# Attention scores as tiles of 128 queries of one head, two heads on TensorE's row halves

## The chip, the cores and the metric

One core of a Trainium2 chip runs the whole program. The metric is the device time of one execution in microseconds, the median of three runs. A change of 0.2% is about what such a measurement can tell from no change.

## The reference

Three layers follow each other, all in float32:

```python
# attention: q, k, v of (batch 4, heads 8, sequence 576, width 64)
scores = (1/8) * q @ k.T
mask = block_i >= block_j            # blocks of 64: a query sees its own block and those before
attn = softmax(where(mask, scores, -1e9))
x = (attn @ v), heads side by side   # 2304 tokens x 512
# squared-ReLU layer, 512 -> 2048 -> 512
r = max(x @ w_in, 0);  x2 = (s * r * r + b) @ w_out
# top-1 mixture of 8 experts, 512 -> 1024 -> 512, chosen by modality-biased logits
out = gate * (max(x2 @ w1[e], 0) @ w2[e])
```

Products with full float32 accuracy are made of three passes: either operand is split into a high and a low part of the reduced type fp32r (names ending in h and l), and high by high, high by low and low by high are summed in PSUM (`PASSES`).

## The kernel before, in words

`attention` (line 21) works through 16 units; one unit is a batch's pair of heads. For each unit q and k come in as rows, are transposed on TensorE (`transpose4`, line 82; the last 64 rows in `tails`, line 113), copied out by ScalarE as the high part and subtracted by VectorE to the low part (`q_high`, `k_transpose`, `flush`).

The 576 queries of a unit are nine blocks of 64. `scores(u, i)` (line 123) makes one tile for block i: its 128 rows are 64 queries of the first head and the same 64 of the second. The stationary operand is block-diagonal (head 0's queries on rows 0 to 63, head 1's on rows 64 to 127, zeros elsewhere), so one full-array product gives both heads. The tile ends at the block's own edge, n = 64 (i + 1) keys, and needs no mask. The first two blocks are float32 products (line 137), the others three passes of fp32r of at least 256 columns (line 140), the ninth in two parts of 288. VectorE takes the row maximum (line 142), ScalarE the exponential with its sum (line 147).

```python
LAGS = (1, 5, 7)        # steps to normalise, p_transpose, pv
NPBUF = 6
BANKS_0 = (4, 3, 1)     # PSUM banks: scores, transposes, outputs
```

A step is one block. In step t `normalise` (line 151) for the block before takes the reciprocals on VectorE and multiplies on GpSimd (line 160); `p_transpose` (line 162) for the block five steps back turns the probabilities on TensorE (line 179) and ScalarE copies them out (line 185); `pv` (line 189) for a group of blocks makes the output, either head on one half of TensorE's columns (line 202), and ScalarE copies it out (line 204). A program-wide scheduler puts the instructions of all of this in an order for each engine.

`SquaredRelu` fills the rest. In the first stage its weights are converted, a chunk every few steps (`CONV`; VectorE lines 329 to 331, ScalarE 363, GpSimd 335). From step `PIECE_0` on, pieces of its first layers (`hidden`, line 376; `project`, line 391, sums in `pxa`) go between the attention's steps, one each `PIECE_D` steps, for tokens whose attention is done. What is left of the layer, the routing and the experts follow after the attention.

Of the kernel before, what the change touches and what calls it, by code (L numbers as in the profile page):

```python
# [20 lines left out]
def attention(nc, tc, ctx, ps, ident, q, k, v, xT_d):  # L21
    """x^T = softmax(mask(q k^T / 8)) v, written to xT_d[(head d), (batch s)]; a
    generator that yields (units finished) after each block of queries it emits.

    One unit is a batch's pair of heads.  Rows of the score tiles are a block of
    64 queries of either head (block-diagonal stationary), so a tile ends at its
    block's edge and needs no mask.
    """
    B, H, S, D = q.shape
    NB = S // D  # L30
# [14 lines left out]
    qb, qf = [], []  # L45
    for par in range(2):
        qq = []
        for nm in ("qh", "ql"):
# [3 lines left out]
        qb.append(qq)  # L52
        t = fix.tile([P, 2, 2, D], F32, name=f"qf{par}")
        nc.gpsimd.memset(t, 0.0)
        qf.append(t)
    st = {}
    todo = []

    def load(u, which):
# [4 lines left out]
        for nm, src in which:  # L64
            t = (vp if nm == "v" else raw).tile([P, 5, 2, D], F32, name=f"raw_{nm}", tag=nm)
            for hh in range(2):
                nc.sync.dma_start(t[:, 0:4, hh], src[b, h0 + hh, 0:512].rearrange("(c p) d -> p c d", p=P))
            ps.last["load"] = nc.sync.dma_start(t[0:D, 4], src[b, h0:h0 + 2, 512:].rearrange("h p d -> p h d"))
            ts.append(t)
# [18 lines left out]
    def q_high(u, src, blocks):  # L88
        skip = max(2 - blocks.start, 0)
        for hh in range(2):  # L90
            r = slice(hh * D, hh * D + D)
            a = src[r].rearrange("p (i d) -> p i d", d=D)
            if skip:
                nc.scalar.activation(qf[u % 2][r, :, hh], a[:, 0:skip], AF.Copy, scale=0.125)
                a = a[:, skip:]
            oh, ol = (t[r, blocks.start + skip - 2:blocks.stop - 2, hh] for t in qb[u % 2])
            nc.scalar.activation(oh, a, AF.Copy, scale=0.125)
            low(True, ol, a, oh)

    def q_transpose(u):  # L100
        q_high(u, transpose4(st[u]["raw"][0]), slice(0, 8))

    def k_transpose(u):
        kh = kt.tile([P, S], F32R, name="kh", tag="kh")
        kl = kt.tile([P, S], F32R, name="kl", tag="kl")
        kf = kt.tile([P, P], F32, name="kf", tag="kf")
        st[u]["k"] = (kh, kl, kf)
        t = transpose4(st[u]["raw"][1])
        nc.scalar.copy(kf, t[:, 0:P])
        nc.scalar.copy(kh[:, 0:512], t)  # L110
        low(False, kl[:, 0:512], t, kh[:, 0:512])

    def tails(u):
# [4 lines left out]
        q_high(u, t[:, 0:D], slice(8, 9))  # L118
        kh, kl, _ = st[u]["k"]
        nc.scalar.copy(kh[:, 512:], t[:, D:2 * D])  # L120
        low(False, kl[:, 512:], t[:, D:2 * D], kh[:, 512:])

    def scores(u, i):
        kh, kl, kf = st[u]["k"]
        qh, ql = qb[u % 2]
        n = (i + 1) * D
        pr = pp.tile([P, 640], F32, name="p", tag="p")
        if i % 2 == 0:
            nc.gpsimd.memset(pr[:, n:n + D], 0.0)
        parts = [(0, n)] if i < 8 else [(0, 288), (288, 288)]  # L130
        nm = small.tile([P, 2], F32, name="nm", tag="nm")
        sm = small.tile([P, 2], F32, name="sm", tag="sm")
        scs = []
        for e, (k0, w) in enumerate(parts):
            sc = ps.s.tile([P, 512], F32, name="sc", tag="s")
            if i < 2:
                nc.tensor.matmul(sc[:, 0:w], qf[u % 2][:, i].rearrange("p h d -> p (h d)"), kf[:, 0:w],
                                 start=True, stop=True)
            for j, (a, kk) in enumerate(((qh, kh), (qh, kl), (ql, kh)) if i >= 2 else ()):
                nc.tensor.matmul(sc[:, 0:max(w, 256)], a[:, i - 2].rearrange("p h d -> p (h d)"),  # L140
                                 kk[:, k0:k0 + max(w, 256)], start=(j == 0), stop=(j == 2))
            ps.last["max"] = nc.vector.tensor_reduce(nm[:, e:e + 1], sc[:, 0:w], AX.X, ALU.max, negate=True)  # L142
            scs.append(sc)
        if len(parts) == 2:
            nc.vector.tensor_tensor(nm[:, 0:1], nm[:, 0:1], nm[:, 1:2], ALU.min)
        for e, (k0, w) in enumerate(parts):
            ps.last["exp"] = nc.scalar.activation(pr[:, k0:k0 + w], scs[e][:, 0:w], AF.Exp, bias=nm[:, 0:1],  # L147
                                                  accum_out=sm[:, e:e + 1])
        st[u][i] = (pr, sm, len(parts))

    def normalise(u, i):
        n = (i + 1) * D
        pr, sm, k_ = st[u][i]
        rc = small.tile([P, 1], F32, name="rc", tag="rc")
        if k_ == 2:
            nc.vector.tensor_scalar(rc, sm[:, 0:1], sm[:, 1:2], 1e-9, ALU.add, ALU.add)
        else:
            nc.vector.tensor_scalar_add(rc, sm[:, 0:1], 1e-9)
# [3 lines left out]
    def p_transpose(u, blocks):  # L162
# [23 lines left out]
        for i in blocks:  # L186
            st[u].pop(i)
# [36 lines left out]
    for t in range(len(seq) + LP + 1):  # L224
# [26 lines left out]
        if i == 3:  # L251
            pv(u, 0)
# [956 lines left out]
```

## Time and profile before

| what | value |
|---|---|
| time, median of 3 runs | 957.22 us (956.84 to 957.99) |
| span of the profiled execution | 951.0 us |
| TensorE (PE) busy | 902.0 us, 95% |
| VectorE (DVE) busy | 593.8 us, 62% |
| ScalarE (ACT) busy | 521.1 us, 55% |
| GpSimd (POOL) busy | 252.3 us, 27% |
| last x^T of the attention sent off | 336.1 us |

The profile has no time of its own for this execution beside the span; the rest of the run's time lies before the first and behind the last instruction. Times are from the span's start. PE is TensorE's products, PEld its weight loads. An instruction's duration holds the time in which it drains, so two that follow each other overlap in the profile, and the step from one start to the next tells what it costs in a dense stream.

### The profile page before, as it was taken

To read this page: it belongs to the slowest core of one execution; us is meant where nothing else is said; L and a number is where in the kernel's file an instruction comes from. 1 tells how busy PE (TensorE), PEld (TensorE's weight loads), DVE (VectorE), ACT (ScalarE), POOL (GpSimd) and SP (SyncE) were. 2 spreads that over 40 slices of the span, in tenths; PEclk is the share of its full clock that TensorE was granted. 3 is DMA by queue.
4 is the path that set the end of the run, shared out by engine and by line. 5 is a ranking of instruction groups with operands and counts; after the bars stand their busy time and mean duration, and the time that the engine had idled before them with its cause. 6 is when DMAs were issued, how large, how long until landed. Compare 5 with 4: busy or idle time off the path is not lost. (4 is left out here: it accounts for less than half of the span.)

```text
span 951.0 us, 16300 instructions
## 1 busy us (share of the span) xinstructions
PE 902.0 (95%) x5553; PEld 728.7 (77%) x5553; DVE 593.8 (62%) x1340; ACT 521.1 (55%) x1105; POOL 252.3 (27%) x343
## 2 busy tenths in 40 slices
PE   7979999999999998999999999999779999999995
PEld 5666777888888887789898988887557776776774
DVE  5898886464546278743434444445877887676762
ACT  6878785566766443322222222224267877776763
POOL 4566674232323224200000000005251222222110
PEclk9999999999999999999999999999889999999998
DMA  6565643322220255200011222115162696637400
GB/s 146 153 155 138 177 131 80 89 57 67 73 70 27 79 180 163 71 21 26 20 32 40 64 67 67 45 46 202 42 246 84 238 372 234 225 121 255 170 24 25
DMA packets 105061, 107.50 MB, mean 113 GB/s; under 512 B 62359, under 2 KB 78249, under 8 KB 104971
## 3 DMA queue, kind: packets, MB, share of 16 engines
q1 hardware_dynamic: 101163, 94.45, 31.7%
q0 software_dynamic: 3808, 11.94, 3.5%
q8 instruction: 46, 0.75, 0.3%
q14 instruction: 44, 0.36, 0.1%
HBM read 139.38 MB, written 17.70 MB: 165 GB/s over the span
## 5 line engine op out<-in xcount | busy, mean ns | idle before, releaser
L376 PE MATMUL ph<-xh,wih 128*128 128x256 f32 x576 | 163.1, 283 | 0.0
L376 PE MATMUL ph<-xh,wil 128*128 128x256 f32 x576 | 162.5, 282 | 0.0
L376 PE MATMUL ph<-xl,wih 128*128 128x256 f32 x576 | 162.3, 282 | 0.0
L160 POOL TENSOR_TENSOR p<-p,rc 128x64 f32<-128x64 f32 (+2 forms) x144 | 111.8, 783 | 135.8 <-DVE rc L159 68.7
L380 ACT ACTIVATE r<-ph 128x512 f32<-128x512 f32 x72 | 43.0, 598 | 184.1 <-PE ph L376 158.0
L381 DVE SCALAR_TENSOR_TENSOR r<-r,sc 128x512 f32<-128x512 f32 x72 | 56.9, 792 | 112.8 <-ACT r L380 108.9
L376 PEld LDWEIGHTS ph<-xh,wih 128*128 128x128 f32 x576 | 109.1, 189 | 3.6 <-ACT r L380 0.9
L376 PEld LDWEIGHTS ph<-xl,wih 128*128 128x128 f32 x576 | 109.2, 190 | 2.2
L376 PEld LDWEIGHTS ph<-xh,wil 128*128 128x128 f32 x576 | 109.3, 190 | 0.2
L142 DVE TENSOR_REDUCE nm<-sc 128x1 f32<-128x288 f32 (+8 forms) x160 | 70.7, 450 | 53.7 <-PE sc L140 43.3
L147 ACT ACTIVATE p<-sc,nm 128x288 f32<-128x288 f32 (+8 forms) x160 | 80.6, 507 | 23.2 <-DVE nm L142 9.3
L885 DVE TENSOR_TENSOR w2l<-raw,w2h 128x1024 fp32r<-128x1024 f32 x62 | 79.9, 1303 | 14.6 <-ACT w2h L883 13.2
L391 PE MATMUL px<-woh,gh 128*128 128x512 f32 x200 | 82.6, 413 | 3.3 <-ACT gh L384 3.3
L391 PE MATMUL px<-woh,gl 128*128 128x512 f32 x200 | 79.3, 397 | 0.8 <-DVE gl L385 0.8
L885 DVE TENSOR_TENSOR w1l<-raw,w1h 128x1024 fp32r<-128x1024 f32 x58 | 70.0, 1226 | 15.7 <-ACT w1h L883 14.3
L391 PE MATMUL px<-wol,gh 128*128 128x512 f32 x200 | 79.3, 396 | 0.0
L883 ACT CAST w1h<-raw 128x1024 fp32r<-128x1024 f32 x64 | 65.7, 1050 | 22.1 <-PE ph L924 20.8
L883 ACT CAST w2h<-raw 128x1024 fp32r<-128x1024 f32 x64 | 66.6, 1051 | 12.4 <-PE py L940 11.7
L384 ACT ACTIVATE gh<-r,sc 128x512 fp32r<-128x512 f32 x72 | 52.1, 724 | 35.9 <-DVE r L381 35.7
L179 PE MATMUL tp<-ident,p 128*128 128x128 f32 x400 | 66.3, 281 | 5.3 <-POOL p L160 3.7
L894 POOL DMA_INDIRECT xr<-x_d,gidx_e x2 | 2.3, 1132 | 254.1 <-DMA raw<-in_moe_w_dram 253.8
L385 DVE SCALAR_TENSOR_TENSOR gl<-r,sc,gh 128x512 fp32r<-128x512 f32 x72 | 56.0, 778 | 20.8 <-ACT gh L384 20.4
(269 smaller groups left out, 2018.9 us busy)
## 6 DMA issues: line engine op xcount, KB each, us to landing
raw<-in_moe_w_dram SPq DMA_DIRECT2D x172, 512.0 KB
wr<-in_moe_w_in_dram SPq DMA_DIRECT2D x16, 512.0 KB
wr<-in_moe_w_out_dram SPq DMA_DIRECT2D x16, 512.0 KB
xr<-xT_d SPq DMA_DIRECT2D x15, 512.0 KB
x_d<-row SPq DMA_DIRECT2D x18, 256.5 KB
xT_d<-x SPq DMA_DIRECT2D x16, 288.0 KB
raw_q<-in_q_dram SPq DMA_DIRECT2D x32, 128.0 KB
raw_k<-in_k_dram SPq DMA_DIRECT2D x32, 128.0 KB
```

The lines of the kernel that those rows point to most:

```text
L142: ps.last["max"] = nc.vector.tensor_reduce(nm[:, e:e + 1], sc[:, 0:w], AX.X, ALU.max, negate=True)
L147: ps.last["exp"] = nc.scalar.activation(pr[:, k0:k0 + w], scs[e][:, 0:w], AF.Exp, bias=nm[:, 0:1], accum_out=sm[:, e:e + 1])
L160: ps.last["scale"] = nc.gpsimd.tensor_mul(pr[:, 0:n], pr[:, 0:n], rc.to_broadcast([P, n]))
L179: nc.tensor.transpose(t[:, e * P:(e + 1) * P], st[u][i][0][:, c * P:(c + 1) * P], ident)
L376: nc.tensor.matmul(ph[:, e], self.wi[p][w][:, c, e * P:(e + 1) * P], x[a][:, c], start=(n == 0), stop=(n == 3 * KC - 1))
L380: nc.scalar.activation(r, ph, AF.Relu)
L381: nc.vector.scalar_tensor_tensor(r, r, self.sc[:, 0:1], r, ALU.mult, ALU.mult)
L384: nc.scalar.activation(gh, r, AF.Identity, bias=self.sc[:, 1:2])
L385: nc.vector.scalar_tensor_tensor(gl, r, self.sc[:, 1:2], gh.bitcast(F32), ALU.add, ALU.subtract)
L391: self.nc.tensor.matmul(px, g[a][:, e, t * P:(t + 1) * P], self.wo[p][w][:, e], start=(first and e == 0 and n == 0), stop=(last and e == 1 ...
L883: self.nc.scalar.copy(ws[0][c], r)
L885: eng.tensor_sub(ws[1][c], r, ws[0][c].bitcast(F32))
```

## The change

The 576 queries become four tiles of 128 queries and one of 64. A tile of 128 (j = 0 to 3) is of one head: head 0 uses rows 0 to 63 of the array, head 1 rows 64 to 127, each with its own PSUM bank, and both are handled by one maximum and two exponentials. Keys run to n = 128 (j + 1); the later 64 queries of a tile see them all, the earlier 64 must not see the last 64, so a product of two small bf16 constants adds -1e30 there. The last 64 queries stay as before, one block-diagonal tile, now with one maximum and one exponential over both parts. A unit is 5 steps instead of 9. The float32 blocks, the copies for them, and the zeros behind odd tiles are gone; fp32r products of 128 columns are new. Output products and transposes have the same columns in another layout. Some copies of transposed probabilities go to VectorE from unit 4 on. A score tile takes two banks, so the FFN's `pxa` shares the bank of the outputs, and its sum is made in two pieces.

```diff
-            t = fix.tile([P, NB - 2, 2, D], F32R, name=f"{nm}{par}")
+            t = fix.tile([P, 2, D], F32R, name=f"{nm}{par}")
+    mq = fix.tile([P, P], BF16, name="mq")
+    mk = fix.tile([P, D], BF16, name="mk")
+    for hh in range(2):
+        nc.gpsimd.memset(mq[hh * D:hh * D + 1, 0:D], -1e30)
+        nc.gpsimd.memset(mk[hh * D:hh * D + 1], 1.0)
...
     def q_transpose(u):
-        q_high(u, transpose4(st[u]["raw"][0]), slice(0, 8))
+        qh = kt.tile([P, SF], F32R, name="qh", tag="qh")
+        ql = kt.tile([P, SF], F32R, name="ql", tag="ql")
+        st[u]["q"] = (qh, ql)
+        t = transpose4(st[u]["raw"][0])
+        nc.scalar.activation(qh, t, AF.Copy, scale=0.125)
+        low(True, ql, t, qh)
...
+    def scores(u, j):
+        kk, qq = st[u]["k"], st[u]["q"]
+        n = (j + 1) * P
+        pr = pp.tile([P, 2, 512], F32, name="p", tag="p")
...
+        sc = ps.s.tile([P, 2, 512], F32, name="sc", tag="s")
+        if j < NT:
+            for e, (a, w) in enumerate(PASSES):
+                for hh, r in enumerate(half):
+                    nc.tensor.matmul(sc[:, hh, 0:n], qq[a][r, j * P:(j + 1) * P], kk[w][r, 0:n],
+                                     start=(e == 0), stop=False)
+            for hh, r in enumerate(half):
+                nc.tensor.matmul(sc[:, hh, n - D:n], mq[r], mk[r], start=False, stop=True)
+            ps.last["max"] = nc.vector.tensor_reduce(nm, sc[:, :, 0:n], AX.X, ALU.max, negate=True)
+            for hh in range(2):
+                ps.last["exp"] = nc.scalar.activation(pr[:, hh, 0:n], sc[:, hh, 0:n], AF.Exp, bias=nm[:, hh:hh + 1],
+                                                      accum_out=sm[:, hh:hh + 1])
+            st[u][j] = (pr[:, :, 0:n], pr, sm)
         else:
...
+            ps.last["max"] = nc.vector.tensor_reduce(nm[:, 0:1], sc[:, :, 0:w_], AX.XY, ALU.max, negate=True)
...
-        ps.last["scale"] = nc.gpsimd.tensor_mul(pr[:, 0:n], pr[:, 0:n], rc.to_broadcast([P, n]))
+        ps.last["scale"] = nc.gpsimd.tensor_mul(pr, pr, rc.rearrange("p (g o) -> p g o", o=1).to_broadcast([P, g, n]))
...
-LAGS = (1, 5, 7)
-NPBUF = 6
+LAGS = (1, 3, 4)
+NPBUF = 4
 PTBUF = 1
-BANKS_0 = (4, 3, 1)
-P_COPY = lambda nc, i: nc.scalar.copy
+BANKS_0 = (2, 3, 1)
+P_COPY = lambda nc, u, j, e: nc.vector.tensor_copy if u >= 4 and j in (2, 4) and e else nc.scalar.copy
...
-                px = self.ps_x.tile([P, D], F32, name="pxa", tag="x")
+                px = self.ps_x.tile([P, D], F32, name="pxa", tag="o")
                 for p in range(n):
+                    if p == 2:
+                        yield blk
...
-BANKS_A = (3, 2, 1)
+BANKS_A = (2, 2, 1)
-CONV = [8 + 4 * n for n in range(19)]
-PIECE_0 = 50
-PIECE_D = 2.8
+CONV = [4 + 2 * n for n in range(19)]
+PIECE_0 = 26
+PIECE_D = 1.2
```

How it moves instructions: first TensorE in the first stage, transposes of probabilities (tp) and score products (sc), before:

```order
L179 MATMUL tp<-ident,p 128x128 x4
L140 MATMUL sc<-kh,qh_136 128x320
L140 MATMUL sc<-kl,qh_136 128x320
L179 MATMUL tp<-ident,p 128x128
L140 MATMUL sc<-kh,ql_138 128x320
L140 MATMUL sc<-kh,qh_136 128x384
```

The same place of the program after the change (mq and mk are the mask's constants):

```order
L188 MATMUL tp<-ident,p 128x128 x8
L134 MATMUL sc<-kh,qh 128x256 x2
L134 MATMUL sc<-kl,qh 128x256 x2
L134 MATMUL sc<-kh,ql 128x256 x2
L137 LDWEIGHTS mq
L137 MATMUL sc<-mk,mq 128x64
L137 LDWEIGHTS mq
L137 MATMUL sc<-mk,mq 128x64
L188 MATMUL tp<-ident,p 128x128 x4
L188 MATMUL tp<-ident,p 64x128
L134 MATMUL sc<-kh,qh 128x384 x2
```

Before, transposes and scores are all products on the full array; now the pairs (x2, one a head) and the mask stand on halves of its rows, between transposes on all rows and, for the tile's last 64 keys, one on half of the columns.

Second, ScalarE at the program's start (qf, qh, kf, kh: copies of q and k; p: exponentials), before:

```order
L97 ACTIVATE qh_136<-te 64x64 x2
L120 CAST kh<-te 128x64
L94 ACTIVATE qf_146<-tw 64x2x64
L97 ACTIVATE qh_142<-tw 64x6x64
L94 ACTIVATE qf_146<-tw 64x2x64
L97 ACTIVATE qh_142<-tw 64x6x64
L147 ACTIVATE p,sm<-sc,nm 128x64
```

And after:

```order
L118 ACTIVATE qdh_144<-te 64x64 x2
L121 CAST kh<-te 128x64
L140 ACTIVATE p,sm<-sc,nm 128x128 x2
L100 ACTIVATE qh<-tw 128x512
L140 ACTIVATE p,sm<-sc,nm 128x256 x2
```

The second unit's q copies stood ahead of the first exponential; now they stand behind it.

## Rows read from the trace of the kernel before

**Rows 1.** The page's head.

```profile
span 951.0 us, 16300 instructions
```

**Rows 2.** Busy time by stretch: us of the stretch, each engine, clock, DMA share, GB/s.

```profile
0.00:30.00 30.00, 23.56 (x135) 17.70 (x136) 18.83 (x71) 21.93 (x74) 15.20 (x37) 1.00 0.52 119
30.00:95.00 65.00, 56.86 (x391) 42.86 (x390) 57.41 (x173) 53.76 (x170) 41.53 (x68) 0.97 0.61 161
95.00:158.00 63.00, 59.19 (x421) 47.13 (x420) 50.84 (x153) 47.41 (x146) 41.98 (x66) 1.00 0.53 145
158.00:345.00 187.00, 186.77 (x1274) 153.96 (x1273) 94.42 (x279) 113.92 (x316) 53.80 (x96) 1.00 0.24 70
```

**Rows 3.** TensorE in order of time, saturated stage: start, us, instruction, count.

```profile
204.62 0.39 PE L140 MATMUL sc<-kl,qh 128*128 128x512 f32 x1
204.85 0.39 PE L140 MATMUL sc<-kh,ql 128*128 128x512 f32 x1
205.08 0.60 PE L179 MATMUL tp<-ident,p 128*128 128x128 f32 x4
...
205.65 0.29 PE L140 MATMUL sc<-kl,qh 128*128 128x288 f32 x1
205.78 0.29 PE L140 MATMUL sc<-kh,ql 128*128 128x288 f32 x1
...
212.22 0.33 PE L137 MATMUL sc<-kf,qf 128*128 128x64 f32 x2
212.39 0.50 PE L179 MATMUL tp<-ident,p 128*128 128x128 f32 x3
...
213.04 0.87 PE L202 MATMUL o<-pt,raw_v 128*64 128x256 f32 x8
213.85 0.66 PE L179 MATMUL tp<-ident,p 128*128 128x128 f32 x4
...
214.46 0.28 PE L140 MATMUL sc<-kl,qh 128*128 128x256 f32 x1
214.58 0.28 PE L140 MATMUL sc<-kh,ql 128*128 128x256 f32 x1
```

**Rows 4.** TensorE in order of time where two 64-row transposes interrupt FFN products.

```profile
180.36 0.38 PE L376 MATMUL ph<-xh,wih 128*128 128x256 f32 x1
180.67 0.27 PE L116 MATMUL te<-ident,raw_q 64*128 64x64 f32 x1
180.78 0.22 PE L116 MATMUL te<-ident,raw_k 64*128 64x64 f32 x1
180.94 0.38 PE L376 MATMUL ph<-xl,wih 128*128 128x256 f32 x1
181.16 0.28 PE L376 MATMUL ph<-xh,wil 128*128 128x256 f32 x1
```

**Rows 5.** TensorE's weight loads in order of time.

```profile
65.47 0.47 PEld L179 LDWEIGHTS tp<-ident,p 128*128 128x128 f32 x4
65.90 0.19 PEld L140 LDWEIGHTS sc<-kh,qh 128*128 128x128 f32 x1
```

**Rows 6.** ScalarE in order of time at the start.

```profile
10.76 0.27 ACT L94 ACTIVATE qf<-tw 64x128 f32<-64x128 f32 x1 [2.19 <-PE tw L85]
...
12.09 0.32 ACT L147 ACTIVATE p<-sc,nm 128x64 f32<-128x64 f32 x1
```

**Rows 7.** VectorE in order of time at the start.

```profile
9.25 0.41 DVE L142 TENSOR_REDUCE nm<-sc 128x1 f32<-128x64 f32 x2
```

**Rows 8.** Waits from 30 to 95 us: us in total, times, longest.

```profile
PEld tp L179 <- POOL p L160: 4.4, 6, 2.1
...
PEld sc L140 <- ACT p L147: 2.7, 3, 1.4
```

**Rows 9.** Groups by line, span to 350 us: busy us, mean ns; idle before.

```profile
L159 DVE RECIPROCAL rc<-rc 128x1 f32<-128x1 f32 x144 | 22.3, 157 | 2.3
```

**Rows 10.** The page's groups, GpSimd's normalisation.

```profile
L160 POOL TENSOR_TENSOR p<-p,rc 128x64 f32<-128x64 f32 (+2 forms) x144 | 111.8, 783 | 135.8 <-DVE rc L159 68.7
```

More of the change, by code (lines that the diff above doesn't have):

```diff
@@ L117, in tails @@
                                 st[u]["raw"][n][0:D, 4].rearrange("p h d -> p (h d)"), ident[0:D, 0:D])
[L118 to L130, printed above, removed]
+        for hh, r in enumerate(half):
+            oh, ol = (x[r, hh] for x in qd[u % 2])
+            nc.scalar.activation(oh, t[r, 0:D], AF.Copy, scale=0.125)
+            low(True, ol, t[r, 0:D], oh)
@@ L131, in scores @@
+        kh, kl = st[u]["k"]
+        nc.scalar.copy(kh[:, SF:], t[:, D:2 * D])
+        low(False, kl[:, SF:], t[:, D:2 * D], kh[:, SF:])
+    def scores(u, j):
+        kk, qq = st[u]["k"], st[u]["q"]
+        n = (j + 1) * P
+        pr = pp.tile([P, 2, 512], F32, name="p", tag="p")
         nm = small.tile([P, 2], F32, name="nm", tag="nm")
         sm = small.tile([P, 2], F32, name="sm", tag="sm")
[L133 to L143, printed above, removed]
@@ new lines, in normalise, with p_transpose @@
+    def normalise(u, j):
+        pr, _, sm = st[u][j]
+        g = sm.shape[1]
+        rc = small.tile([P, 2], F32, name="rc", tag="rc")[:, 0:g]
+        nc.vector.tensor_scalar_add(rc, sm, 1e-9)
+        nc.vector.reciprocal(rc, rc)
+        n = pr.shape[2]
+        ps.last["scale"] = nc.gpsimd.tensor_mul(pr, pr, rc.rearrange("p (g o) -> p g o", o=1).to_broadcast([P, g, n]))
+    def p_transpose(u, j):
+        _, pr, _ = st[u][j]
+        grp = int(j >= 2)
+        if j == 2 * grp:
+            st[u]["pt", grp] = pt.tile(([P, 2, 2, 256], [P, 5, 2, 320])[grp], F32, name=f"pt{grp}", tag=f"pt{grp}")
@@ L186, in p_transpose @@
-        for i in blocks:
-            st[u].pop(i)
+            r = lst[0].shape[1]
+            for i, a in enumerate(lst):
+                nc.tensor.transpose(t[0:r, i * P:(i + 1) * P], a, ident)
+            src = t[0:r, 0:len(lst) * P].rearrange(how, **kw)
+            P_COPY(nc, u, j, e)(o, src)
+        st[u].pop(j)
     def pv(u, grp):
@@ L198, in pv @@
         for c in cs:
-            first, kr = max(0, 2 * c - 4 * grp), P if c < 4 else D
-            for hh in range(2):
-                r = slice(hh * D, hh * D + D)
-                nc.tensor.matmul(o[r, first * D:n], vt[0:kr, c, hh], p[0:kr, first:, c, r],
+            first, kr = max(0, c - 2 * grp) * P, P if c < NT else D
+            for hh, r in enumerate(half):
+                nc.tensor.matmul(o[r, first:n], vt[0:kr, c, hh], p[0:kr, c, hh, first:],
                                  start=(c == 0), stop=(c == cs[-1]))
@@ L217, in attention @@
     flush()
-    seq = [(u, i) for u in range(NU) for i in range(NB)]
+    seq = [(u, j) for u in range(NU) for j in range(NT + 1)]
     def at(t):
@@ L1129 @@
     B, H, S, _ = q.shape
-    per = H // 2 * S // 64
+    per = H // 2 * (S // P + 1)
     begun = (B - 1) * S // TB + MORE
```

135 lines of the change are left out of this document (55 added, 80 removed).

## The prediction

> **What bounds the kernel now.** I read the busy time by stretch first, then TensorE's order of time inside one stretch, then the waits. The attention with the work beside it ends near 345 us of a span of 951.0 us [rows 1, 2]; the other 606 us are code that the change leaves alone. Within the 345 us the table by stretch shows two stages. Up to 95 us TensorE is idle for 30 - 23.6 = 6.4 us and 65 - 56.9 = 8.1 us, and VectorE (57.4 of 65) and ScalarE (53.8 of 65) are nearly as busy as it is. From 95 us on it is idle for 3.8 us of 63, then for 0.2 us of 187. So in the second stage the time is the length of TensorE's own stream: whatever an instruction adds to or takes from that stream is paid in full. Only about 18 us of idle time exist at all that better overlap could remove. The profiled execution has a span of 951.0 us; the median run took 957.2 us, so 6.2 us lie around the span, and I add my differences to 957.2.
>
> **Part 1: the score products.** An instruction's price in the stream is the step from its start to the next one's start, since its own duration contains its drain. Those steps [rows 3]: 0.23 us for 512 columns of fp32r, 0.13 for 288, 0.12 for 256; I interpolate 0.146 (320), 0.178 (384) and 0.20 (448). The two float32 blocks cost 0.17 for the 64 columns (two instructions) and, at 0.11 each, 0.22 for the 128. One unit before: 6 x 0.12 + 3 x 0.146 + 3 x 0.178 + 3 x 0.20 + 3 x 0.23 + 6 x 0.13 + 0.17 + 0.22 = 4.2 us.
>
> After, each of the first four tiles has three passes of two heads, each head on 64 rows. If the two halves run side by side, a pair costs one instruction. No row shows two row halves at once. The nearest rows are the output products, where two heads use two column halves: eight instructions (four of 256 columns, four of 128) begin at 213.04, and the transposes behind them at 213.85, 0.81 us later; one after another, at 0.11 us per 128 columns, they would need 1.3 us [rows 3]. I take side by side, with one after another as the far bound. For 128 columns of fp32r there is no row either. The lower bound is half of the 256-column step, 0.06, the upper one the float32 price, 0.22; I take 0.11, the step between weight loads of 128 columns (four from 65.47 to 65.90) [rows 5], because a product can't be quicker than its own weights. So a unit after: 3 x 0.11 + 3 x 0.12 + 3 x 0.178 + 3 x 0.23 = 1.9, the last block 6 x 0.13 = 0.78, and four mask pairs. A mask product is 64 columns of bf16; the 64-column float32 step (0.085) is its upper bound, 0.02 the lower (a quarter of that), I take 0.05 a pair, 0.2 in all. Sum 2.9 us. Gain: 1.3 us a unit, 16 units: **-20.3 us**.
>
> **Part 2: changes of tile shape.** This is what the diff hides. The order shows score blocks on 64-row tiles standing between transposes and FFN products on full tiles. Counted along TensorE's order up to the last output product, the tile shape changes 129 times before and 274 times after: 145 more. The trace prices a change: two small transposes on 64 rows (te) stand alone in a stream of 256-column products. From the product before them (180.36) to the second one after them (181.16) it takes 0.80 us; the same four in one shape would take 2 x 0.12 + 2 x 0.11 = 0.46 [rows 4]. One look at where: te starts 0.31 after the product instead of 0.12, and the first product after te needs 0.22 instead of 0.12, because its weights couldn't be loaded ahead. So 0.34 us there and back, 0.17 a change: 145 x 0.17 = **+24.7 us**. The bounds are 0.14 and 0.20 (20 to 29 us), as either transpose may be worth 0.06 or 0.14.
>
> The two parts together are +4.4 us: TensorE has fewer columns to stream and drains more often, and the one eats the other.
>
> **Part 3: the start.** ScalarE's first exponential runs at 12.09 us although its maxima were taken from 9.25 on, because ScalarE stands at the next unit's q copy (10.76, after 2.19 us of idleness) [rows 6, 7]. In the new order the exponentials come ahead of that copy. I take **-1.5 us**; the bounds are 0 and -2.4.
>
> **Part 4: waits in the first stage.** They are TensorE's transposes waiting for GpSimd's normalisation (4.4 us) and its scores waiting for an exponential to free a bank (2.7 us) [rows 8]. The change halves the small instructions: 80 reciprocals of 0.157 us instead of 144 and 80 normalisations instead of 144 at 0.78 us, though these are longer [rows 9, 10], four fewer q and k copies a unit on ScalarE, no padding memsets. Half of the 11.9 us of idle time from 30 to 158 us goes, I estimate: **-6 us**. The bounds are -13 (all of it, with the tails that busy time hides) and +6 (a wait of 0.25 us more at each of the first 26 steps).
>
> Costed at nothing: copies that move to VectorE from unit 4 on, since VectorE is busy for 94 of 187 us there [rows 2]; the bank shared by the output products and the FFN's sums, since TensorE has other work to do ahead (if that is missing, a wait is up to 24 x 0.23 = 5.6 us); DMAs, which are the same; transposes and output products, the same columns in another layout. What is late next is TensorE itself.
>
> Sum: -20.3 + 24.7 - 1.5 - 6 = -3.1 us, **954 us**.
>
> **The rivals.**
> (a) *The halves get in each other's way* (slower). If two weight loads of 128 columns follow each other at 0.11 us, a pair can't be quicker than 0.22: the first three tiles cost 0.66 each and the last 0.69, 2.7 us in place of 1.9. The first FFN piece comes at step 26 of five a unit, so 10.8 of the 16 units lie in the second stage, and there it is +8.3 us: 962 us; it decides as soon as tiles narrower than 512 columns gain nothing from pairing. For it: the step of 0.108 between weight loads is as long as a short product's; against: the output products' loads come in pairs as well and don't show. The Trainium skill, "TensorE: Matmul & The Clock Gate", Part 3, bears on this: it says that row tiles do run concurrently, but gives 3.07 times the speed for four row tiles of 512 columns, which by an estimate from that figure makes a pair 1.3 times one product, +0.6 us a unit and about 960 us here. No run here shows it.
> (b) *No overlap at all.* Each pair costs two: +1.9 us a unit, 20.6 us over these 10.8 units and some 5 in the first stage: 980 us. For it: nothing but that no row shows row halves.
> (c) *The bigger steps starve TensorE* (slower). Two score tiles of two banks replace four of one, and a tile is free only after one maximum over both heads and two exponentials. If that costs 0.25 us at each step instead of saving, part 4 is +6 instead of -6 and the time 966 us; it decides in the first stage alone.
> (d) *Overlap goes well and a change costs its lower bound.* Part 4 at -11 and part 2 at 20.3: -12.5, 945 us.
> (e) *It cancels.* Part 4 at about -3: 957 us.
>
> **How the numbers follow.** My forecast (952 to 955) has a chance of 0.33, (d) 0.18, (e) 0.15, (a) 0.13, (c) 0.13, (b) 0.08. A difference of 0.2% is 1.9 us, about what a measurement of this kernel can tell from no change. So faster 0.51, same 0.15, slower 0.34. The range reaches from below (d) to behind (c), 942 to 969, and leaves out (b) and some tails.
>
> **What would show it.** In the new profile pairs of score products should begin within hundredths of a microsecond of each other, 0.12 or 0.23 us before the next pair, and 0.22 flat would be (a). Each score block should begin about 0.1 us late and the first transposes after it too. TensorE's idle time ahead of the first FFN piece should shrink, while the attention behind it should take no less of TensorE's time per unit. I am wrong if the saturated stage itself becomes clearly shorter, because then a change of shape costs less than te shows, or if the first stage becomes longer.

## The result and the profile after

| | before | after |
|---|---|---|
| time, median | 957.03 us (4 runs, 956.05 to 957.99) | 966.25 us (4 runs, 964.09 to 967.32) |
| span of the profiled execution | 951.0 us | 965.7 us |
| TensorE busy | 902.0 us | 899.6 us |
| last x^T of the attention sent off | 336.1 us | 354.0 us |

The kernel became slower: 1.0094 times the time of before, with an interval of 1.0080 to 1.0109, so 9.2 us. The time lies in the forecast's range, but on the other side of no change than the forecast.

Busy time by stretch after the change (us of the stretch, then for each engine busy us and instructions, then granted clock, DMA share, GB/s); the first four answer to [rows 2]:

```profile
0.00:30.00 30.00, 21.20 (x145) 15.03 (x147) 15.18 (x37) 17.76 (x54) 9.47 (x24) 1.00 0.52 117
30.00:95.00 65.00, 54.03 (x418) 36.20 (x415) 54.03 (x114) 49.36 (x142) 38.29 (x30) 0.95 0.60 163
95.00:158.00 63.00, 57.98 (x430) 45.52 (x428) 45.45 (x97) 38.42 (x102) 29.98 (x31) 1.00 0.44 116
158.00:345.00 187.00, 183.20 (x1355) 145.07 (x1354) 95.52 (x203) 109.25 (x284) 48.64 (x39) 1.00 0.22 63
345.00:430.00 85.00, 75.26 (x448) 63.46 (x447) 61.81 (x81) 27.88 (x45) 23.68 (x16) 0.98 0.43 134
```

The last of these stretches for the kernel before, where the attention gives way to the next layer:

```profile
345.00:430.00 85.00, 80.79 (x497) 70.25 (x495) 57.68 (x92) 28.36 (x46) 20.16 (x14) 0.98 0.33 105
```

The first number behind the length is TensorE's. Subtracted from the length it gives the idle time, and the difference to before [rows 2] is +2.4 us up to 30, +2.8 to 95, +1.2 to 158, +3.6 to 345, +5.5 to 430, and +1.6 behind that: 17.1 us more in which TensorE stands, against 2.4 us less in which it works. That is the 14.7 us between the two spans. (It is more than the 9.2 us of the medians, because the profiled execution of before was a quick one: the 6.2 us that the forecast took to lie around the span are no such thing; after the change a profiled span of 965.7 belongs to a run of 967.32 us, 1.6 us around it, which puts the profiled one of before at some 952.6 us. So about 5 us of the 14.7 are two ordinary executions that differ. No record of a product of the attention or the FFN is missing that could explain it: the page has 5713 of TensorE after and 5553 before, and the 160 between them are ten for each of 16 units, 38 for scores and masks instead of 28.) ScalarE, VectorE and GpSimd have less to do than before in the first stages, and yet TensorE waits more.

TensorE in order of time after the change, at the start and in the dense stage (start, us, instruction, count; x2 is a pair, one product on either row half; in brackets idle time ahead, and what ended it):

```profile
9.97 0.45 PE L92 MATMUL tw<-ident,raw_q 128*128 128x128 f32 x1 [2.55 <-DMA raw_q<-in_q_dram]
10.35 0.79 PE L134 MATMUL sc<-kh,qh 64*128 64x128 f32 x4
...
229.21 1.04 PE L188 MATMUL tp<-ident,p 128*128 128x128 f32 x8
230.18 0.39 PE L134 MATMUL sc<-kh,qh 64*128 64x256 f32 x2
230.40 0.28 PE L134 MATMUL sc<-kl,qh 64*128 64x256 f32 x2
230.52 0.29 PE L134 MATMUL sc<-kh,ql 64*128 64x256 f32 x2
230.65 0.20 PE L137 MATMUL sc<-mk,mq 64*128 64x64 bf16 x2
230.78 0.39 PE L377 MATMUL ph<-xh,wih 128*128 128x256 f32 x1
231.00 0.28 PE L377 MATMUL ph<-xl,wih 128*128 128x256 f32 x1
...
236.31 0.39 PE L134 MATMUL sc<-kl,qh 64*128 64x512 f32 x2
236.54 0.40 PE L134 MATMUL sc<-kh,ql 64*128 64x512 f32 x2
```

In the dense stage the forecast's picture holds. A pair costs what one product costs: 0.12 us for 256 columns (230.40 to 230.52) and 0.23 for 512 (236.31 to 236.54), as for one full-array product in [rows 3]. Its duration, 0.28 and 0.39 us, is that of one product too, so its two halves start together. The changes of shape are there too. Eight transposes at 0.11 would be done after 0.88 us; the block begins after 0.97. Its first pair takes 0.22 instead of 0.12, and the first FFN product behind it also 0.22. The mask pair takes 0.13, its drain included. From the last transpose to that product's successor the 256-column block costs 0.09 + 0.60 + 0.10 = 0.79 us; the forecast's terms give 3 x 0.12 + 0.05 + 2 x 0.17 = 0.75.

The start shows where part 3 went. ScalarE's first exponential:

```profile
12.08 0.37 ACT L140 ACTIVATE p<-sc,nm 128x128 f32<-128x128 f32 x1 [3.87 <-DVE nm L138]
```

The first exponential runs at 12.08 us, as before (12.09, [rows 6]). It no longer stands behind the next unit's q copy on ScalarE, but the scores themselves now stand behind the next unit's q transposes on TensorE (9.97 above), and these wait 2.55 us for their rows to arrive. In the kernel before the first maximum was taken at 9.25 [rows 7], so its scores ran ahead of that load. The wait moved one queue up.

TensorE's products and what they waited for from 30 to 95 us (total, times, longest), before:

```profile
PE tp L179 <- POOL p L160: 3.1, 4, 1.9
PE sc L140 <- ACT p L147: 2.0, 2, 1.1
PE sc L137 <- ACT p L147: 1.2, 2, 0.7
```

And after:

```profile
PE tp L188 <- POOL p L162: 5.8, 6, 1.7
PE sc L134 <- ACT p L140: 3.4, 3, 1.6
PE tp L188 <- DVE pt L190: 1.4, 1, 1.4
```

These are the waits of products; [rows 8] has those of the weight loads (PEld) ahead of them, and of those the first grew from 4.4 us to 8.0. So the wait for the normalisation nearly doubled, that for an exponential hardly changed (3.2 us before, 3.4 after), and the third is new: a transpose waits for a copy that the change moved to VectorE. GpSimd's groups (busy us, mean ns, idle before), the answer to [rows 10]:

```profile
L162 POOL TENSOR_TENSOR p<-p,rc 128x256 f32<-128x256 f32 (+4 forms) x80 | 99.4, 1246 | 211.8 <-DVE rc L160 185.6
```

Fewer instructions and less work in all (99.4 us for 111.8), but each takes 1.25 us instead of 0.78, and a transpose can start only when its whole tile is normalised. A second link of the same chain grew, VectorE's addition of 1e-9 to the sums, which stands ahead of the reciprocal. Two of these additions, and what GpSimd did beside the first (start, us):

```profile
36.52 1.28 POOL L336 TENSOR_TENSOR wil<-f,wih 128x512 fp32r<-128x512 f32 x1
36.58 1.26 DVE L159 TENSOR_SCALAR rc<-sm 128x2 f32<-128x2 f32 x1 [1.01 <-POOL p L162]
41.70 0.16 DVE L159 TENSOR_SCALAR rc<-sm 128x2 f32<-128x2 f32 x1
```

The first ends 0.03 us after GpSimd's instruction. Of the 64 two-column additions, the 22 that overlapped a GpSimd instruction took 0.78 us on average, the other 42 took 0.16. Up to 158 us this adds 10.7 us to the chains of 12 tiles. How much of it TensorE waits for, no run separates.

Then the hand-over to the next layer. The queue of DMA issues on SyncE, before (start, us, line, what is sent; part_d and xT_d are stores of the FFN's pieces and of the attention, wr the weights of what is left of the FFN, called the next layer here):

```profile
322.65 0.32 SPq L207 DMA_DIRECT2D xT_d<-x  x1
323.06 1.00 SPq L320 DMA_DIRECT2D wr<-in_moe_w_in_dram  x2
336.09 0.34 SPq L207 DMA_DIRECT2D xT_d<-x  x1
```

And after:

```profile
332.89 0.32 SPq L210 DMA_DIRECT2D xT_d<-x  x1
351.07 0.32 SPq L419 DMA_DIRECT2D part_d<-rowa  x1
353.56 0.38 SPq L321 DMA_DIRECT2D wr<-in_moe_w_in_dram  x1
354.02 0.47 SPq L210 DMA_DIRECT2D xT_d<-x  x1
```

The FFN's pieces go one each 1.2 steps of 80 now (one each 2.8 of 144 before), and more of their work stands ahead of the attention's end, in TensorE's stream and in the queue. In the queue a store of theirs waits for its rows, and from 332.9 to 351.1 us nothing is issued at all. What SyncE's queue waits for from 250 to 430 us (total, times, longest):

```profile
SPq L419 <- ACT rowa L418: 35.3, 5, 17.8
```

The same wait came to 25.2 us before. The next layer's first weights are asked for at 353.6 us instead of 323.1, 30 us later, and from 345 to 430 TensorE stands for 9.7 us instead of 4.2.

But the queue alone does not set these times. The attention's last output products on TensorE, what the first weight load waited for in SyncE's queue once that store was gone, and two of TensorE's waits from 345 to 430 us:

```profile
351.10 2.42 PE L205 MATMUL o<-pt,raw_v 128*64 128x320 f32 x20 [0.51 <-ACT rowa L418]
SPq L321 <- PE o L205: 2.0, 1, 2.0
PE ph L377 <- ACT xh L315: 3.3, 1, 3.3
PE ph L377 <- POOL wil L336: 1.9, 2, 1.0
```

The weight load waits for those output products, which end at 353.5, and so does the last x^T, sent off at 354.0. The longest wait of this stretch, 3.3 us, is not for weights but for that x^T: it is stored, loaded again and cast (xh) before the next layer's first product can start. What covers this way is the pieces' work that is left. Behind its last output product the attention of before left 48 products of 512 columns of the pieces and some shorter ones, and nothing waited for xh; after the change it is 24, and they are done 3.3 us too soon.

### The profile page after: what moved, and what is told of

Read it like the earlier page. It is cut to its first block, busy times and chain, and to the rows that moved or that the text cites. A ratio compares the mean times of both kernels' runs of the same rounds, so it can differ in the third digit from the quotient of the medians.

```text
span 965.7 us, 16003 instructions
## 1 busy us (share of the span) xinstructions
PE 899.6 (93%) x5713; PEld 713.2 (74%) x5713; DVE 592.7 (61%) x1124; ACT 501.5 (52%) x985; POOL 228.3 (24%) x203
## 5 line engine op out<-in xcount | busy, mean ns | idle before, releaser
L162 POOL TENSOR_TENSOR p<-p,rc 128x256 f32<-128x256 f32 (+4 forms) x80 | 99.4, 1246 | 211.8 <-DVE rc L160 185.6
L140 ACT ACTIVATE p<-sc,nm 128x128 f32<-128x128 f32 (+3 forms) x128 | 66.5, 527 | 25.4 <-DVE nm L138 17.6
L188 PE MATMUL tp<-ident,p 128*128 128x128 f32 (+1 forms) x400 | 62.1, 281 | 14.1 <-POOL p L162 8.0
L138 DVE TENSOR_REDUCE nm<-sc 128x2 f32<-128x256 f32 (+1 forms) x64 | 52.3, 817 | 25.5 <-PE sc L137 25.4
L188 PEld LDWEIGHTS tp<-ident,p 128*128 128x128 f32 (+1 forms) x400 | 43.7, 140 | 23.8 <-POOL p L162 11.1
```

Source lines behind the costliest of these rows:

```text
L138: ps.last["max"] = nc.vector.tensor_reduce(nm, sc[:, :, 0:n], AX.X, ALU.max, negate=True)
L140: ps.last["exp"] = nc.scalar.activation(pr[:, hh, 0:n], sc[:, hh, 0:n], AF.Exp, bias=nm[:, hh:hh + 1], accum_out=sm[:, hh:hh + 1])
L162: ps.last["scale"] = nc.gpsimd.tensor_mul(pr, pr, rc.rearrange("p (g o) -> p g o", o=1).to_broadcast([P, g, n]))
L188: nc.tensor.transpose(t[0:r, i * P:(i + 1) * P], a, ident)
```

## The experiments

Each ran beside the kernel before; the ratio is to runs of that kernel.

### TensorE's stream: pairs and changes of shape

**Score products on the full array (e1).** The queries are padded with zeros to 128 rows, so each head needs a product of its own on the full array; shapes change 168 times instead of 274. The copies of q and their low parts become two instructions each.

```diff
-nc.tensor.matmul(sc[:, hh, 0:n], qq[a][r, j * P:(j + 1) * P], kk[w][r, 0:n],
+nc.tensor.matmul(sc[:, hh, 0:n], qq[a][:, hh, j * P:(j + 1) * P], kk[w][:, 0:n],
...
-nc.tensor.matmul(sc[:, hh, n - D:n], mq[r], mk[r], start=False, stop=True)
+nc.tensor.matmul(sc[:, hh, n - D:n], mq, mk, start=False, stop=True)
```

> The changed kernel with its score products on the full array: each head's queries stand in a stationary operand of 128 rows whose other half is zeros, so the two heads follow each other and no score block changes TensorE's tile shape (168 changes of shape instead of 274). Theory S (a change of shape costs 0.17 us, a pair on row halves costs one product): 106 fewer changes save 18 us, the unpaired products (a unit: 6 x 0.11 + 6 x 0.12 + 6 x 0.178 + 6 x 0.23 = 3.8 us in place of 1.8) cost 32 us; net +14 us over all units and +10 us over those that TensorE bounds, so 972 to 980 us against 966. Rival N (a change of shape costs nothing, the loss lies elsewhere): only the products count, +22 to +32 us, 988 to 998 us. Rival P (pairs don't overlap): only the changes count, 948 to 954 us.

Measured: 976.21 us, ratio 1.0207 (1.0185 to 1.0229), 10 us over the change. By the forecast's prices the lost pairing costs 16 x 1.9 = 30 us and four more mask products a unit 3, and 106 fewer changes at 0.17 give 18 back: +15, less what falls into idle time. So the pairing is real and worth more than the drains that it brings. The price of a change is bounded only loosely by this: at 0.12 us the same sum gives +21, and how much falls into idle time isn't known.

**The kernel before with its tails on full tiles (e7).** q's, k's and v's last 64 rows are filled up with zeros, so the two small transposes and the last output products use all rows: 83 changes of shape in place of 129. The two transposes are 64 columns longer.

```diff
+            nc.gpsimd.memset(t[D:, 4], 0.0)
...
-            nc.tensor.transpose(t[:, n * D:n * D + D],
-                                st[u]["raw"][n][0:D, 4].rearrange("p h d -> p (h d)"), ident[0:D, 0:D])
+            nc.tensor.transpose(t[:, n * P:n * P + P],
+                                st[u]["raw"][n][:, 4].rearrange("p h d -> p (h d)"), ident)
...
-            first, kr = max(0, 2 * c - 4 * grp), P if c < 4 else D
+            first, kr = max(0, 2 * c - 4 * grp), P
```

> The kernel before with fewer changes of tile shape: the last 64 rows of q, k and v are filled up to 128 with zeros, so that their transposes and the last output products run on 128 rows (83 changes instead of 129; the transposes are 64 columns longer). Theory S: 46 x 0.17 = 8 us less in the stream and 1.6 us more for the longer transposes, of which the part behind 95 us shows in full: 951 to 953 us against 956 to 957. Rival N (a change costs nothing): 957 to 959.

Measured: 952.12 us, ratio 0.9948 (0.9930 to 0.9966): 5 us faster, 0.11 us for each change taken out (0.07 to 0.15 by the interval), in spite of 48 more small memsets on GpSimd. This is faster than either kernel, and in this kernel the cost of part 2 shows by itself. Its trace has the place of [rows 4] without the changes. The line that stands ahead of [rows 4] in the kernel before:

```profile
179.63 0.80 PE L202 MATMUL o<-pt,raw_v 128*64 128x192 f32 x6
```

And the same place in this run, again behind output products:

```profile
179.65 0.39 PE L377 MATMUL ph<-xh,wih 128*128 128x256 f32 x1
179.88 0.27 PE L117 MATMUL te<-ident,raw_q 128*128 128x128 f32 x1
179.99 0.27 PE L117 MATMUL te<-ident,raw_k 128*128 128x128 f32 x1
180.02 0.36 PE L377 MATMUL ph<-xl,wih 128*128 128x256 f32 x1
180.22 0.28 PE L377 MATMUL ph<-xh,wil 128*128 128x256 f32 x1
```

From the first product to the second behind the transposes it takes 0.57 us instead of 0.80: 0.23 there and back, 0.12 a change.

**The last transpose of a unit on all columns (e4).** In the change, 257 changes of shape in place of 274.

```diff
+            nc.gpsimd.memset(pf[:, S:S + D], 0.0)
...
-            jobs.append(([pr[:, SF:S]], out[0:D, NT, :, q0:q0 + D], "p (h n) -> p h n", dict(h=2)))
+            jobs.append(([pr[:, SF:SF + P]], out[:, NT, :, q0:q0 + D], "p (h n) -> p h n", dict(h=2)))
```

> The changed kernel with the last transpose of a unit on all 128 columns (64 of them zeros) instead of 64, which takes 17 changes of shape away and adds a memset on GpSimd. Theory S: 17 x 0.17 = 3 us less, 962 to 964 us. Rival N: no difference, 966 us.

Measured: 965.65 us, ratio 1.0095 (1.0073 to 1.0116). No difference from the change can be told; 3 us were expected. A miss, and by itself inconclusive.

### The spacing of the FFN's pieces

**Pieces later (e2).**

```diff
-PIECE_D = 1.2
+PIECE_D = 1.45
```

> The changed kernel with the FFN's pieces 1.45 steps apart instead of 1.2, so that about ten of the 50 are left when the attention ends instead of two. Theory H (8 of the lost us come at the hand-over: the next layer's weight loads start at 354 us instead of 323, and too little product work is left to cover their conversion): the first weight load of the next layer comes 15 to 25 us earlier and the time falls by 5 to 9 us, to 957 to 961. Rival S alone (the loss is TensorE's stream in the attention): the same products in another order, 966 within 2 us.

Measured: 959.75 us, ratio 1.0031 (1.0017 to 1.0045). One number gives back some 6 of the 9 us (6.5 by the medians, 6.0 by the ratios). SyncE's queue in this kernel:

```profile
332.48 0.38 SPq L321 DMA_DIRECT2D wr<-in_moe_w_in_dram  x1
332.96 0.46 SPq L210 DMA_DIRECT2D xT_d<-x  x1
```

And its busy time by stretch:

```profile
30.00:95.00 65.00, 54.91 (x394) 37.19 (x390) 53.34 (x113) 47.85 (x140) 36.80 (x29) 0.87 0.60 163
95.00:158.00 63.00, 58.01 (x429) 44.46 (x428) 42.04 (x96) 38.97 (x105) 30.05 (x32) 0.94 0.44 116
...
345.00:430.00 85.00, 79.15 (x490) 69.26 (x489) 60.70 (x75) 29.54 (x47) 20.86 (x15) 0.98 0.33 100
```

The weights are asked for 21 us sooner than in the change, so is the attention's end, and 72 products of the pieces are left behind it. The idle time from 345 to 430 falls from 9.7 to 5.9 us, and no wait for xh is left in it. This profiled execution is the slowest of twelve (965.99 us); the granted clock of the first two rows, 0.87 and 0.94, comes up below.

**The kernel before with its pieces sooner (e3).**

```diff
-PIECE_D = 2.8
+PIECE_D = 2.4
```

> The kernel before with the FFN's pieces 2.4 steps apart instead of 2.8, so that they end with the attention. Theory H: the next layer's weight loads come later and less product work covers them, the time rises by 4 to 9 us to 961 to 966. Rival S alone: 957 within 2 us.

Measured: 965.62 us, ratio 1.0098 (1.0066 to 1.0130), as much as the whole change loses, without any of its scores. In its trace:

```profile
158.00:345.00 187.00, 186.44 (x1254) 154.55 (x1253) 93.14 (x277) 111.46 (x312) 49.86 (x95) 1.00 0.20 56
345.00:430.00 85.00, 70.75 (x442) 60.51 (x440) 60.04 (x81) 29.04 (x48) 23.96 (x17) 0.94 0.41 129
```

TensorE is full from 158 to 345 us and then stands for 14.3 us instead of 4.2. The first weights of the next layer go out at 342.8 us, the last x^T at 355.6 instead of 336.1, and behind the attention's last output product no product of a piece is left: 8.5 of the 14.3 us are one wait for xh. So the hand-over is shown from both sides.

**Pieces later still (e6).**

```diff
-PIECE_D = 1.2
+PIECE_D = 1.7
```

> The changed kernel with the FFN's pieces 1.7 steps apart. Theory H: at 1.45 the conversion is covered as well as in the kernel before, so that more pieces behind the attention bring 0 to 2 us, 958 to 960. If the hand-over isn't what e2 changed but pieces harm the attention's steps, the time falls again by 4 us or more, to 956 or less.

Measured: 964.89 us, ratio 1.0077 (1.0048 to 1.0106); 958 to 960 were expected, a miss. The weights go out at 309.7 us now, but from 95 to 345 us TensorE stands for more:

```profile
95.00:345.00 250.00, 236.88 (x1760) 186.65 (x1760) 157.33 (x325) 149.73 (x389) 90.14 (x77) 1.00 0.37 103
```

That is 13.1 us, against 7.7 us with 1.45 (242.30 of 250 busy). The pieces are also what TensorE does while the attention's own chain isn't ready; spread thinner, they run out as a cover. The spacing has an optimum between two losses.

### The attention's own waits, and TensorE's clock

Some 3 us of the version with the pieces later (e2) are left. Seven kernels look for them.

**A longer lag (e5)**: e2 with one more step between the normalisation and its transposes.

```diff
-LAGS = (1, 3, 4)
-NPBUF = 4
+LAGS = (1, 4, 5)
+NPBUF = 5
```

> The kernel of e2 with the transposes of the probabilities four steps behind their scores instead of three, the outputs five instead of four, and five buffers for the probabilities. Theory W (what is left of the loss is the first stage, where TensorE's transposes wait for GpSimd's normalisation, which now comes in pieces of up to 1024 columns): those waits go, TensorE's idle time from 30 us to the first FFN product falls from 10 us to under 8, and the time by 2 to 3 us against 959.8. Rival S (what is left is the stream with its changes of shape): the same time within 1 us.

Measured: 961.07 us, ratio 1.0049 (1.0028 to 1.0069): no gain, a miss. TensorE's idle time from 30 to 95 us did fall, to 7.2 us, with a granted clock of 0.92 there.

**Full tails in the change (e8)**: e2 with the edits of e4 and e7, 202 changes of shape.

> The kernel of e2 with the same filling up, and with the last transpose of a unit on 128 columns: 202 changes of shape instead of 265. Theory S: 63 x 0.17 = 11 us less in the stream, 1.6 us more for longer transposes, of which two thirds show: 953 to 955 us against 959.8. Rival N: 960 to 962.

Measured: 961.84 us, ratio 1.0052 (1.0032 to 1.0072), a miss: what gave 5 us in the kernel before gives none here.

**Its zeros from VectorE (e11)**: both memsets moved.

```diff
-            nc.gpsimd.memset(t[D:, 4], 0.0)
+            nc.vector.memset(t[D:, 4], 0.0)
```

> Leaves nothing out. The change with the pieces later and the tails on full tiles (202 changes of shape, measured 961.84), but its zeros (four small instructions a unit) written by VectorE instead of GpSimd. Theory M: the missing gain of 6 us was lost because those memsets stand in GpSimd's queue ahead of normalisations: the wait of transposes for GpSimd falls from 8.6 us to 6.5 or less and the time to 954 to 957. Rival I: the saved drains fall where TensorE waits anyway: time 960 to 962 again.

Measured: 964.32 us, ratio 1.0073 (1.0047 to 1.0100). Theory M falls: the wait for GpSimd did become shorter, 6.9 us after 8.6, and the time did not. It is longer than rival I said, too.

**One normalisation a head (e9)**: e2, with each normalisation of 128 queries in two.

```diff
-        ps.last["scale"] = nc.gpsimd.tensor_mul(pr, pr, rc.rearrange("p (g o) -> p g o", o=1).to_broadcast([P, g, n]))
+        for h in range(g):
+            ps.last["scale"] = nc.gpsimd.tensor_mul(pr[:, h], pr[:, h], rc[:, h:h + 1].to_broadcast([P, n]))
```

> Leaves nothing out. The change with the pieces later (PIECE_D 1.45), and each normalisation of a 128-query tile as two GpSimd instructions, one a head, so that the transposes of the first head need not wait for the second. Open is where the rest of the loss (959.75 against 957.03) lies. Theory G: TensorE's transposes wait for GpSimd's normalisation because one instruction is now 0.6 to 1.9 us long: that wait falls from 6.5 us (8 times) to about 4 and the time by 2 to 3 us, to about 957. Rival T: the total of GpSimd's work sets the wait, not its grain; 64 more instructions lengthen it: the wait stays at 6 us or more and the time at 959 to 962.

Measured: 957.89 us, ratio 1.0013 (1.0000 to 1.0026). Its group on GpSimd:

```profile
L163 POOL TENSOR_TENSOR p<-p,rc 128x128 f32<-128x128 f32 (+2 forms) x144 | 113.8, 812 | 175.3 <-DVE rc L160 117.2 <-ACT p L140 32.2 <-ACT kh L108 5.7
```

More work in all (113.8 us for 99.4), in shorter pieces, and TensorE's wait for it falls from 6.5 to 4.3 us, as theory G says. The ratios of e2 and e9 overlap at their ends, so the gain of some 2 us is likely rather than certain.

**The second head's normalisation on VectorE (e10)**, from e2.

```diff
+        for h in range(g):
+            en = nc.vector if h else nc.gpsimd
+            ps.last["scale"] = en.tensor_mul(pr[:, h], pr[:, h], rc[:, h:h + 1].to_broadcast([P, n]))
```

> Leaves nothing out. The change with the pieces later (PIECE_D 1.45), the first head's normalisation on GpSimd, the second head's on VectorE, side by side. Theory G (TensorE waits for the normalisation): the wait for it (6.5 us in eight waits) falls to 2 to 3 us in all, and the time to 955 to 957. Rival V: VectorE, 57 of 65 us busy in the first stage of the kernel before, is then what is late: waits for its copies and low parts take the place of those for GpSimd, time 959 to 963.

Measured: 965.91 us, ratio 1.0094 (1.0073 to 1.0115), worse than rival V said. The wait for GpSimd is still 5.9 us, although GpSimd does less. From 30 to 95 us:

```profile
30.00:95.00 65.00, 54.92 (x376) 36.62 (x377) 57.97 (x126) 46.08 (x138) 31.46 (x29) 0.85 0.61 163
```

VectorE is at 58.0 us of 65, and the granted clock at 0.85.

**The same split at the change's own spacing (e13)**, the edit of e9 with `PIECE_D = 1.2`.

> Leaves nothing out. The change at its own spacing (PIECE_D 1.2), with only each 128-query normalisation as two GpSimd instructions, one a head. Theory G (grain is a cause of its own, worth the 2 us seen between 959.75 and 957.89): 963 to 965 in place of 966.25, and TensorE's wait for GpSimd falls from 8.0 us to about 5. Rival H (the hand-over alone sets the time here, and what the attention gains is lost again behind its stores): 966 to 967, with the first weight load of the next layer still after 352 us.

Measured: 966.76 us, ratio 1.0098 (1.0079 to 1.0117). Rival H: while the hand-over is late, a shorter wait in the attention isn't seen in the time (the wait for GpSimd fell from 8.0 to 6.2 us); the first weights still go out at 352.5 us. e4's miss, at the same spacing, fits in.

**Split and full tails together (e14).**

> Leaves nothing out. Pieces later, normalisation one a head, and tails on full tiles (about 60 fewer changes of shape than 957.89 had). Theory G: the gain of the full tails was hidden behind waits for GpSimd, and comes back now that these are shorter: 953 to 955. Rival K: TensorE's clock eats it; the first stage has the same work in less time of TensorE, so it waits more and falls to the lower clock more often: mean granted clock 0.978 or less and 958 to 962.

Measured: 960.71 us, ratio 1.0039 (1.0026 to 1.0053), with a mean clock of 0.978, as rival K says.

What these share shows in the granted clock. Each execution comes with its mean over the span: 0.984 for the kernel before, 0.983 for the change and for e7 and e15, 0.981 for e9, 0.979 for e2, and 0.978, 0.977, 0.978, 0.975 and 0.978 for e5, e8, e10, e11 and e14. Among executions of one and the same kernel the time falls with it by 0.55 us for 0.001 (209 executions of 17 kernels, each kernel about its own mean). By that slope e2's 0.005 is worth 2.7 us of its 2.8 us in the means, e14's 0.006 is 3.3 of 4.0, e8's 4.0 of 5.2, e11's 5.2 of 7.0; of e10's 9.2 it is 3.2, and of the change's own 9.2 only 0.8. The lower clock lies in the first stages, as the rows of e2 and e10 say: 0.87 and 0.85 there, where the kernel before has 0.97 [rows 2], while from 158 us on it is full. Both rows are of executions slower than their kernel's median. What it costs can be read once without the scatter: up to the first FFN product the change, e2 and e6 run the same code. The change and e6, at 0.95 from 30 to 95 us, get there at 94.5 and 93.6 us; e2's profiled execution, at 0.87, at 99.2, with no more idle time on TensorE (10.1 us, against 11.0 and 9.4). What sets off one more stretch at the lower level, the rows don't tell. The idle time doesn't: from 30 to 95 us it is 7.2 to 11.4 us in e5, e8, e10, e11 and e14, and 9.5 to 9.8 in e7, e12 and e15, whose mean clock is 0.983. So the clock is a cause of some of these last microseconds; that it is the cause of all of them is read from the scatter of the runs, as no kernel here changed the clock alone. And why the tails' memsets, or a longer lag, bring more of these stretches is open.

### A version faster than both

**e7 with its pieces later (e12) and sooner (e15).**

```diff
-PIECE_D = 2.8
+PIECE_D = 2.95
```

> Leaves nothing out. The kernel before with its tails on full tiles (83 changes of shape, measured 952.12) and the pieces a little later (PIECE_D 2.95 in place of 2.8), to see whether the best of these kernels stands at the best spacing. Theory H (hand-over to the next layer): the weights of the next layer start earlier than at 2.8, but that wait was not the bound there: 951 to 953. Rival C: the attention's own waits lose cover first, as with the change at 1.7: 953 to 956.

> Leaves nothing out. The kernel before with tails on full tiles and PIECE_D 2.7 in place of 2.8 (952.12; 954.81 at 2.95). Theory H (hand-over): the first weight load of the next layer moves from 320.5 to some 325 us, the wait before the routing grows by 1 to 2 us: 953 to 955. Rival C (cover): the pieces, earlier, cover the attention's waits better, and the hand-over has slack: 950 to 952.

Measured: 954.81 us at 2.95, ratio 0.9979 (0.9968 to 0.9989), and 951.21 us at 2.7, ratio 0.9936 (0.9920 to 0.9952). Later is worse, sooner at least as good. For 2.7:

```profile
95.00:345.00 250.00, 247.00 (x1723) 206.45 (x1722) 148.60 (x443) 162.92 (x465) 98.96 (x186) 1.00 0.32 89
345.00:430.00 85.00, 79.59 (x494) 69.67 (x493) 59.54 (x95) 28.52 (x46) 20.81 (x14) 0.98 0.34 105
```

At 2.95 TensorE is busy for 244.4 of these 250 us, and for 80.0 of the 85. Rival C: between 2.7 and 2.95 it is the cover that pays, and the hand-over has slack. The best kernel of this study keeps the old scores and loses 50 changes of shape.

## Why the prediction was wrong

**What bounds the kernel**: right that the dense stage is TensorE's stream, and wrong in stopping there. "The other 606 us are code that the change leaves alone" is true of the code; but the change sets when that code may begin. That the time lies inside the range is luck: the range reaches that far for rival (c), whose mechanism isn't what happened.

**Part 1** (-20.3 us; its own rows add up to -20.1) holds: pairs at one product's price, 256 and 512 columns as taken. The mask pair is 0.13 us where it ends a block, not 0.05, but most of that is the drain that part 2 counts. Rivals (a) and (b) are out: no 0.22 flat, no double price. With (a) goes the estimate beside it from the Trainium skill ("TensorE: Matmul & The Clock Gate", Part 3), a pair at 1.3 times one product: with two row halves the trace has 1.0. The estimate had taken the ratio of four tiles for two.

**Part 2** (+24.7 us) holds in kind: a block enters 0.09 late, its first pair takes 0.10 more, the first product behind it 0.10 more. The price was read too high, though. The product that begins at 180.36 in [rows 4] stands itself behind output products on half of the columns (179.63, shown at e7), so 0.10 of the 0.31 us to the first transpose belongs to the change ahead of it: e7's trace, without the two changes around the transposes, still has 0.23 us there (179.65 to 179.88). What is left is 0.24 there and back, 0.12 a change; e7's time gives 0.11, and the block's 0.09 + 0.10 + 0.10 for its two changes gives 0.145. So a change costs what the forecast's lower bound says, or less, and part 2 is +16 to +21 us.

Parts 1 and 2 together were to add 4.4 us to TensorE's work; at these prices they add between -4 and +1, and its busy time fell by 2.4 us. They came out better than forecast, and are not where the loss is.

**Part 3** (-1.5 us) failed: the first exponential didn't move, and the start has 2.4 us more idle time. I had looked at the order of ScalarE alone; the scores stood behind a later load on TensorE.

**Part 4** (-6 us) is one of the two steps that turned the sign. I counted instructions, 80 for 144, and took their number for the waiting. But TensorE waits for a chain, and its links became longer: 1.25 us of normalisation for 0.78, and additions that took 0.78 us instead of 0.14 where GpSimd was busy. Idle time from 30 to 158 us grew by 4.0 us, from 11.9 to 16.0, instead of falling by half; e4, at the same spacing, has 15.0, and e3, with the old attention, 10.8. The first stage became longer in this trace (first FFN product at 94.5 us, 91.9 before), which the forecast had named as the sign that it is wrong; but e3, with the code of before up to that product, has 94.0, so this sign isn't clear of the scatter. e9 shows the grain of the normalisation as one part of the longer waits. Rival (c) came within a microsecond of the time, 966, by a mechanism that explains little of it: waits for an exponential grew by 0.2 us from 30 to 95.

**Costed at nothing** is the other, and the larger: the list has the DMAs "which are the same" and says nothing about `PIECE_D`. The transfers are the same, but what they wait for comes later: the attention ends at 354.0 us instead of 336.1, because more of the pieces' work stands ahead of its end, and too little is left behind it to cover the way of the last x^T. e2 puts this at 6 us, e3 makes the same loss in the old kernel. The diff showed the number, 2.8 of 144 steps against 1.2 of 80, and I read it as a change of scale. It nearly is one: sums in two pieces make 50 pieces out of what were 40, so the same work was spread over 78% of the steps before and 75% after, and its first piece comes at 35% and 33%. But in the order of the code 37 of 40 pieces are then given out within the attention's steps, and 49 of 50 after. It is what is left that counts. Two smaller items of the list cost something too: from 95 to 345 us TensorE waits 1.8 us for copies that moved to VectorE and 1.4 us at the bank that the outputs share with `pxa`, of 8.8 us in which it stands there (4.0 before).

**The base**: the 6.2 us around the span are an ordinary spread of runs; it cost the forecast nothing in the difference, but made the profiled idle times of before look typical when they were low.

## What to carry to other kernels

When a change alters the number of steps, converting every spacing that is counted in steps isn't enough: count what is left of the filler when the stage ends, and compare it with the way of the stage's last output through the DMA queues to the next layer's first product. A filler given out too early can be as bad as one given out too late, and the best spacing lies between two losses. Price a wait by the chain that one consumer waits for, not by the number of instructions on the producer. And where a stream changes tile shape, filling small tiles with zeros can be worth more than the columns it adds: it made the kernel before 5 to 6 us faster.

## What the runs showed of the hardware

Two score products on the two row halves start together and cost one: 0.12 us a pair at 256 columns, 0.23 at 512. VectorE's addition of 1e-9 to the sums took 144 ns for one column before, and 376 ns on average for two after:

```profile
L159 DVE TENSOR_SCALAR rc<-sm 128x2 f32<-128x2 f32 x64 | 24.1, 376 | 28.8 <-ACT p L140 26.8 <-POOL p L162 2.0
```

The mean hides two cases: 0.16 us where GpSimd did nothing, and up to 1.43 us, in most cases to some 0.03 us behind the end of GpSimd's instruction, where it did. Additions of one column took 0.14 to 0.15 us in either case. Why two columns wait and one doesn't, no run here shows.

And some executions of the change's versions got a lower granted clock from 30 to 95 us (0.87 in e2, 0.85 in e10) than the kernel before (0.97). With the same code, e2's came to its first FFN product 4.8 us later for it than the change's; I had not counted the clock as a term at all.
